# Attention outputs kept features by tokens through DRAM, with SyncE's queue in program order

## The chip, the cores and the metric

The kernel runs on one core of one Trainium2 chip. The metric is the device time of one execution in microseconds (us). Three runs of the kernel before took 2798.26, 2801.53 and 2804.0 us; their median, 2801.53 us, is the time that the change is measured against. A profile is one further execution under the hardware profiler.

## The reference

One transformer block on 2048 tokens of 576 features, all in float32. Six modulation rows come from a silu of a condition vector and a matrix. The block is attention with 32 heads of 18 features, then a gated unit of 4608 hidden features:

```python
h = _layernorm(x) * (1 + ca) + sa
q, k, v = (h @ wqkv) split into 32 heads of 18
p = softmax(q @ k.T * 18 ** -0.5)
x = x + ga * ((p @ v) laid side by side @ wo)
h = _layernorm(x) * (1 + cb) + sb
x = x + gb * ((sigmoid(h @ w_gate) * (h @ w_up)) @ w_down)
```

## The kernel before

The program has three stages. The first (to about 245 us) normalizes the input, and projects queries, keys and values; queries and keys go to DRAM (`qd`, `kd`) as two float32r parts. The second is attention (to about 1534 us). The third is the gated unit, a Strassen-like scheme of seven products a block in two halves of the tokens.

**Attention** is a loop over 32 units (L1039). A unit `u` is one half of the queries (1024 of them, `half`) and one pair of heads (`p`); it has 16 steps `kt`, one for each 128 keys. A step has four score products of 128 keys by 512 queries (L1084, "t" in the code), each followed by an exponential on ScalarE (L1088), and takes the four value products of the step two before it (`values`, L656), which add up an output `o` of 128 rows: four groups of 32 (two heads by two blocks of 512 queries), of which the first 18 rows are features and row 18 (`DH`) is the sum of the exponentials. Between them stand four more score products the other way round (L550, "m"), whose row maxima VectorE takes (L556 to L561). These maxima run ahead: the first "m" for unit `u + 2` comes at step 10 of unit `u` (64 a unit, and 24 ahead at the start). When a unit's maxima are complete, `spread` (L577) transposes them and SyncE writes them into four rows of the queries' tile (`mrows`), so that the score products subtract them.

Two steps make a pair. The order of TensorE's products in a pair is written out by hand in the strings of `STEPS`: "V" is a whole value product of 512 columns, "A" and "B" its two halves, "K" takes the finished output, "G" makes room for one piece of the work on rows (`rows0`, `rows1`), "S" for the spread, "O" for the transposes of the output. A pair whose piece is heavy (18 or 28 more products) takes the order "full"; at steps 2 and 12 the heavy piece is held back. TensorE and ScalarE run in the order written (`tc.manual_schedule`); the other engines' queues, SyncE's among them, are ordered by a planner that works from estimated costs. A queue works in order: an instruction that waits holds what stands behind it.

**Loads of a unit.** At the start of unit `u`, `load_heads(u + 2)` (L499) issues eight DMAs on SyncE's queue: for each of the two heads 54 rows of queries (L514, L517) and 54 rows of keys (L518, L522). The tiles that they overwrite are those of unit `u - 1`.

**A unit's output.** At step 1 of the next unit `taken` (L668) copies `o` to `oT` on ScalarE (L673). At step 2, `outputs` (L676) turns it in four transposes on TensorE (L683), ScalarE copies the result back (L699), VectorE takes 16 inverses a row (L702), and GpSimd scales 2 x 144 elements a row (L705) into `Oa` or `big`, which hold tokens by features.

**Rows.** `project_o` (L761) takes 128 tokens at a time. It turns their features back (L772 and L789, four and one transposes, or three for the second half's tokens), splits them into two float32r parts, and multiplies them by the output weights (L805). The first half's eight blocks of rows go from unit 15 on, with the second layer norm behind them (`first_rows`, L871); the second half's from unit 27 on, with the first 384 features only. The last 192 features of these rows go to DRAM (`oend`) and are turned and multiplied in the gated unit's stage (`last_rows`, L1511, transposes at L1526 and L1534), in which VectorE's order too is by hand.

**Other work in attention.** GpSimd prepares the down-projection's weights (`down_parts`) in units 4 to 14 and moves them by DMAs of its own queue; in units 1 and 3, 2.6 MB of modulation weights are loaded on SyncE's queue (`load_mod`, L126).

Of the kernel before, what the change touches and what calls it, by code (L numbers as in the profile page):

```python
# [15 lines left out]
F32 = mybir.dt.float32  # L16
# [71 lines left out]
def tile_block(ctx, tc, x_in, wqkv, wo, w_gate, w_up, w_down, c_in, w_mod, out):  # L88
# [206 lines left out]
    oend = dram.tile([P, 8, D - DL], F32, name="oend")  # L295
# [338 lines left out]
    Os = [Oa]  # L634
# [33 lines left out]
    def taken():  # L668

        if "whole" in state:  # L670
            half, p, acc = state.pop("whole")
            oT = epool.tile([P, 512], F32, name="oT")
            nc.scalar.copy(oT, acc)  # L673
            state["end"] = (half, p, oT)

    def outputs():  # L676

        if "end" not in state:
            return
        half, p, oT = state.pop("end")  # L680
        tp = bank().rearrange("p (b q) -> p b q", q=P)
        for b in range(4):
            nc.tensor.transpose(tp[:, b, :], oT[:, b * P : (b + 1) * P], ident)  # L683

        yield
        tq = tp.rearrange("p b (j e) -> p j b e", e=32)
        rec = epool.tile([P, 4, 4], F32, name="rec")
        if half == 1 and p == H // 2 - 1:
            nc.vector.reciprocal(rec, tq[:, :, :, DH])
            state["last"] = epool.tile([P, 512], F32, name="oT")[:, 0 : 16 * DH].rearrange("p (t e) -> p t e", t=8)  # L690
            for h in range(2):
                nc.vector.tensor_tensor(
                    state["last"][:, :, h * DH : (h + 1) * DH].rearrange("p (c b) e -> p c b e", c=2),
                    tq[:, 2 * h : 2 * h + 2, :, 0:DH],
                    rec[:, 2 * h : 2 * h + 2, :].unsqueeze(3).to_broadcast([P, 2, 4, DH]),
                    op=ALU.mult,
                )
            return
        nc.scalar.copy(oT, tp.rearrange("p b q -> p (b q)"))  # L699
        yield  # L700
        tq = oT.rearrange("p (b j e) -> p j b e", j=4, e=32)
        nc.vector.reciprocal(rec, tq[:, :, :, DH])  # L702
        for h in range(2):
            f0 = (2 * p + h) * DH
            nc.gpsimd.tensor_tensor(  # L705
                Os[half][:, :, f0 : f0 + DH].rearrange("p (c b) e -> p c b e", c=2),
                tq[:, 2 * h : 2 * h + 2, :, 0:DH],
                rec[:, 2 * h : 2 * h + 2, :].unsqueeze(3).to_broadcast([P, 2, 4, DH]),
                op=ALU.mult,
            )  # L710


# [4 lines left out]
    def load_wo():  # L717
# [31 lines left out]
        for _ in range(4):  # L749
            yield  # L750
# [3 lines left out]
    def project_o(t):  # L754

        wo_h, wo_l, we = weights
        if t <= 8:
            held_rows[:] = temp([P, 2048], F32R), temp([P, 2048], F32)
        T, T_ = held_rows
        if t < 8:  # L760
            xt, full, od = T_[:, 0:D], T_[:, 1024:1536], T_[:, 1536:1664]  # L761
        else:
            T, T_ = T[:, 1024 * (t % 2) : 1024 * (t % 2) + 1024], T_[:, 960 * (t % 2) : 960 * (t % 2) + 960]
            xt, full = T_[:, 0:D], T_[:, D : D + 384]
        nc.gpsimd.dma_start(xt, x_rows[:, t, :])
        src = Os[t // 8][:, t % 8, :]
        n = 4 if t < 8 else DL // P
        oh = T[:, 0 : n * P]
        ol = T[:, 512 : 512 + n * P]
        pt = bank()  # L770
        for i in range(n):
            nc.tensor.transpose(pt[:, i * P : (i + 1) * P], src[:, i * P : (i + 1) * P], ident)  # L772
        if t >= 12:
            nc.vector.tensor_copy(oh, pt[:, 0 : n * P])
            nc.vector.tensor_sub(ol, pt[:, 0 : n * P], oh.bitcast(F32))  # L775
        else:
            full = full[:, 0 : n * P]
            nc.vector.tensor_copy(full, pt[:, 0 : n * P])
            nc.gpsimd.tensor_copy(oh, full)
            nc.gpsimd.tensor_sub(ol, full, oh.bitcast(F32))  # L780
        yield None if t < 8 else "g"
        if t < 8:
            om = T[:, 1024:1152]
            omh = T[:, 1152:1280]
            nc.gpsimd.tensor_copy(
                od.rearrange("p (a e) -> p a e", e=64), src[:, DM:D].unsqueeze(1).to_broadcast([P, 2, 64])
            )
            pt = bank()
            nc.tensor.transpose(pt[:, 0:P], od, ident)  # L789
            nc.vector.tensor_copy(od, pt[:, 0:P])  # L790
            nc.gpsimd.tensor_copy(om[0:64], od[0:64])
            nc.gpsimd.tensor_copy(omh[64:P], od[64:P])
            nc.gpsimd.tensor_sub(om[64:P], od[64:P], omh[64:P].bitcast(F32))
            yield "g"
        for h in range(2):
            cols = slice(h * HALF, (h + 1) * HALF)
            ts_ = []
            for i in range(n):
                a, b = oh[:, i * P : (i + 1) * P], ol[:, i * P : (i + 1) * P]
                ts_ += [(a, wo_h[:, i, cols]), (a, wo_l[:, i, cols]), (b, wo_h[:, i, cols])]  # L800
            if t < 8:
                ts_ += [(om, we[:, 0, cols]), (om, we[:, 1, cols])]
            acc = bank()
            for i, (a, w) in enumerate(ts_):
                nc.tensor.matmul(acc[:, :HALF], a, w, start=i == 0, stop=i == len(ts_) - 1)  # L805
            to = Oa[:, t, :] if t < 8 else xt
            nc.vector.tensor_add(to[:, cols], xt[:, cols], acc[:, 0:HALF])
            yield None if h else "g"
        if t >= 8:
            nc.gpsimd.dma_start(x1p[:, t - 8, :], xt)  # L810
# [64 lines left out]
    def first_rows():  # L875
        yield from load_wo()
        for t in range(8):
            yield from project_o(t)
# [118 lines left out]
    def last_rows_project():  # L997
        for t in range(8, NT):
            yield from project_o(t)

# [33 lines left out]
    manual.enter_context(tc.manual_schedule(engines={mybir.EngineType.PE, mybir.EngineType.Activation}))  # L1034
    follow = []
    rows0 = first_rows()
    rows1 = last_rows_project()
    downs = down_parts()
    for u in range(UNITS):  # L1039
        half, p = divmod(u, H // 2)  # L1040
        qs, ks = heads(u)
        if 0 < u < UNITS - 2:
            load_heads(u + 2)
        if u == H // 2:
            Os.append(big.tile([P, 8, 640], F32, name="big"))
        for kt in range(NT):
# [3 lines left out]
            if kt % 2 == 0:  # L1050
                heavy = state.get("next") == "g"
                hold = heavy and (kt == 2 or kt == 12 and u < UNITS - 1)
                halved = step >= 10 and (hold or not heavy)
                rows = FROM0 <= step < FROM1
                order = two_steps(STEPS["full" if not halved else "rows" if rows else kt if kt in STEPS else "half"])
# [78 lines left out]
    for _ in outputs():  # L1134
        pass
# [375 lines left out]
    def last_rows():  # L1511

        def psum():
            return pd.tile([P, 512], F32, name="d")
# [303 lines left out]
```

## Time and profile before

| what | value |
|---|---|
| runs | 2798.26, 2801.53, 2804.0 us |
| the profiled execution | 2804.88 us |
| its span | 2803.1 us |
| granted TensorE clock, mean | 0.998 |
| TensorE matmul busy | 2771.9 us (99%) |
| VectorE busy | 2306.3 us (82%) |
| ScalarE busy | 1609.3 us (57%) |
| GpSimd busy | 814.6 us (29%) |

The page gives an engine's busy time over the whole span, though the stages differ: ScalarE is nearly full in attention and half idle in the gated unit. Matmul ends are modelled, so a busy share of 99% doesn't say how close TensorE is to its peak; the distance from one value product to the same one a pair later does, since these starts are recorded. "PEld" is TensorE's load of weights, "SPq" SyncE's queue, in which only the issue of a DMA is seen and not its landing. A row of the profile reads: start or count, duration, engine, line, operation, tiles written and read.

### The profile page before, as it was taken

What the parts mean: (1) busy time and instruction counts of PE and PEld (TensorE: products, weight loads), DVE (VectorE), ACT (ScalarE), POOL (GpSimd) and SP (SyncE); (2) the same over time, 40 slices, a digit from 0 to 9 for tenths busy, and PEclk for the clock granted to TensorE, in tenths of its full rate; (3) what the DMA queues carried; (4) which work ended last, traced back from release to release, by engine and by line L of the source; (5) the groups of instructions that cost most, each with busy time, mean ns of one, the idle gap of its engine ahead of it and who ended that gap; (6) DMA issues with size and microseconds to landing.
All of it is one profiled execution on the core that took longest, in us unless ns stands there. A gap on an engine that the chain in (4) does not pass through costs nothing.

```text
span 2803.1 us, 50644 instructions
## 1 busy us (share of the span) xinstructions
PE 2771.9 (99%) x18637; PEld 1847.4 (66%) x18637; DVE 2306.3 (82%) x4370; ACT 1609.3 (57%) x3051; POOL 814.6 (29%) x1077
## 2 busy tenths in 40 slices
PE   7999999999999999999999999999999999999999
PEld 5975444444444444444444888888888888888888
DVE  7278999999998888999883778888898677777777
ACT  3215999999999878999888332333333222222221
POOL 3125207888843111663103222232221100000000
PEclk9999999999999999999999999999999999999999
DMA  5344224444432120232127766667767956566653
GB/s 172 121 157 140 78 61 162 171 169 166 172 133 82 36 58 24 98 106 71 43 68 227 273 222 223 240 213 273 278 245 280 339 195 201 194 200 195 200 195 120
DMA packets 170777, 462.59 MB, mean 165 GB/s; under 512 B 21212, under 2 KB 88032, under 8 KB 160416
## 3 DMA queue, kind: packets, MB, share of 16 engines
q1 hardware_dynamic: 150064, 360.72, 38.4%
q0 software_dynamic: 20464, 98.62, 9.9%
q8 instruction: 147, 2.41, 0.4%
q14 instruction: 102, 0.84, 0.1%
HBM read 281.92 MB, written 176.82 MB: 164 GB/s over the span
## 4 chain that ended last, share of the span: by engine, by line
PE 92%; DVE 4%; DMA 2%; issue 2%; POOL 0%; ACT 0%; SPq 0%; DVEq 0%; ACTq 0%; POOLq 0%
PE x L1225 26%; PE o L656 19%; PE s L1084 12%; PE s L550 11%; PE d L1375 8%; PE d L1307 6%; PE s L336 4%; PE s L805 2%; PE s L389 1%; DMA out_dram<-Oa 1%; DVE mx L556 1%; PE s L683 1%; DMA wq_raw<-in_A_wqkv_dram 1%; DVE w L1215 0%; DVE Oa L1379 0%
## 5 line engine op out<-in xcount | busy, mean ns | idle before, releaser
L1088 ACT ACTIVATE p<-s 128x512 f32<-128x512 f32 x2048 | 1069.1, 616 | 89.2 <-PE s L1084 62.6
L556 DVE TENSOR_REDUCE mx<-s 128x1 f32<-128x512 f32 x1568 | 1000.9, 683 | 101.3 <-PE s L550 75.1
L656 PE MATMUL o<-p,vaug 128*32 128x256 f32 (+1 forms) x5848 | 595.1, 478 | 0.1
L550 PE MATMUL s<-k,q 54*128 54x512 f32 x1920 | 548.6, 434 | 2.0 <-DVE t L775 1.0
L1084 PE MATMUL s<-q,k 56*128 56x512 f32 x1920 | 527.7, 440 | 0.0
L550 PEld LDWEIGHTS s<-k,q 54*128 54x128 f32 x1920 | 273.4, 184 | 231.9 <-DVE mx L561 88.0
L1084 PEld LDWEIGHTS s<-q,k 56*128 56x128 f32 x1920 | 249.8, 184 | 232.1 <-ACT p L1088 72.9
L1225 PE MATMUL x<-k,w 128*128 128x512 f32 x1512 | 370.0, 392 | 0.0
L1225 PEld LDWEIGHTS x<-k,w 128*128 128x128 f32 x1512 | 276.8, 188 | 53.3 <-PE o L656 0.8
L1375 PE MATMUL d<-wd,hh 128*128 128x288 f32 x1248 | 249.9, 295 | 2.4 <-DVE Oa L1379 2.4
L656 PEld LDWEIGHTS o<-p,vaug 128*32 128x32 f32 x5848 | 116.2, 108 | 203.1 <-issue 187.5
L1225 PE MATMUL x<-big,w 128*128 128x512 f32 x1008 | 245.5, 392 | 0.7 <-DVE u L1724 0.7
L1225 PE MATMUL x<-w,w 128*128 128x512 f32 x1008 | 245.3, 391 | 0.0
L1225 PEld LDWEIGHTS x<-big,w 128*128 128x128 f32 x1008 | 185.1, 188 | 37.0 <-DVE u L1724 1.1
L1225 PEld LDWEIGHTS x<-w,w 128*128 128x128 f32 x1008 | 184.3, 188 | 34.5
L1375 PEld LDWEIGHTS d<-wd,hh 128*128 128x128 f32 x1248 | 202.2, 188 | 6.2 <-DVE Oa L1379 3.1
L1375 PE MATMUL d<-wd,hl 128*128 128x288 f32 x624 | 184.3, 295 | 0.0
L1379 DVE TENSOR_TENSOR Oa<-Oa,d 128x288 f32<-128x288 f32 x312 | 136.6, 453 | 55.1 <-PE d L1375 51.2
L561 DVE CUSTOM_DVE_ANT_0 over<-s,over 128x512 f32<-128x512 f32 x240 | 163.9, 683 | 1.3 <-PE s L1084 1.2
L559 ACT ACTIVATE over<-s 128x512 f32<-128x512 f32 x240 | 145.8, 608 | 11.3 <-PE s L550 9.3
L1234 ACT ACTIVATE sg<-x 128x512 f32<-128x512 f32 x36 | 21.6, 599 | 210.2 <-PE x L1225 210.2
L1206 ACT CAST w<-S 128x768 fp32r<-128x768 f32 x71 | 59.4, 836 | 137.8 <-POOL S L1179 136.0
(275 smaller groups left out, 3898.5 us busy)
## 6 DMA issues: line engine op xcount, KB each, us to landing
ws<-w SPq DMA_DIRECT2D x126, 640.0 KB
w<-ws SPq DMA_DIRECT2D x126, 640.0 KB
wd<-wds SPq DMA_DIRECT2D x19, 1152.0 KB
k<-kd SPq DMA_DIRECT2D x60, 360.0 KB
wds<-w POOLq DMA_DIRECT2D x18, 1152.0 KB, 5.2
wtd<-t POOLq DMA_DIRECT2D x32, 576.0 KB, 5.0
wt<-wtd SPq DMA_DIRECT2D x64, 288.0 KB
wd<-wds SPq DMA_DIRECT2D x52, 288.0 KB
```

Of the source, the lines that this page charges most:

```text
L336: nc.tensor.matmul(acc, w, hT[:, t, cols], start=n == 0, stop=n == len(ts_) - 1)
L550: nc.tensor.matmul(sp, qs[rows, qt * P : (qt + 1) * P], ks[rows, at * 512 : (at + 1) * 512], start=True, stop=True,)
L556: nc.vector.tensor_reduce(to, sp, axis=AX.X, op=ALU.max)
L559: nc.scalar.activation(over, sp, AF.Relu)
L561: nc.vector.tensor_tensor_reduce(out=over, in0=sp, in1=over, scale=1.0, scalar=LOWEST, op0=ALU.add, op1=ALU.max, accum_out=mx[:, h * n + q ...
L656: nc.tensor.matmul(acc[32 * j : 32 * j + 32, cols], vaug[:, kt, (2 * p + h) * VW : (2 * p + h) * VW + 32], probs[2 * c + h][:, cols], star ...
L1084: nc.tensor.matmul(sT, ks[rows, kcols], qs[rows, c * 512 : (c + 1) * 512], start=True, stop=True)
L1088: state["exp"] = nc.scalar.activation(pr, sT, AF.Exp, scale=SCALE)
L1225: nc.tensor.matmul(acc[v], w[:, v, a, :], X[s][:, b, :], start=first and n == 0, stop=n == 6, skip_group_check=not first,)
L1307: nc.tensor.matmul(acc, a[:, rows], w[:, k, :], start=n == 0, stop=n == 2)
L1375: nc.tensor.matmul(acc[:, :HALF], a[:, f, rows], w[:, f, cols], start=n == 0, stop=n == 5)
L1379: nc.vector.tensor_add(Oa[:, t, cols], Oa[:, t, cols], acc[:, :HALF])
```

## The change

The output stays features by tokens, and the transposes on both sides of it go.

- `taken` still copies `o` to `oT`. It then stores the four rows of sums in DRAM (`osums`) and loads them as 128 x 16 (`sT`).
- `outputs` is a new generator. From step 2: VectorE inverts the 128 x 16, SyncE stores them in DRAM and loads them spread out, 32 rows for each group (`R`, 128 x 512). From step 6 GpSimd multiplies `R` by `oT`, in place. From step 14 SyncE stores the four groups of 18 rows in `ot`, a DRAM tensor of 576 features by 2048 tokens.
- `load_rows` brings `ot` back as features by tokens into `big`, at units 14, 16, 26 and 27. `rows_parts` splits 128 tokens' columns of it on GpSimd, one block of rows ahead of its products; `project_rows` replaces `project_o`.
- The orders for steps 2 and 4 are taken out of `STEPS`, and heavy pieces are held back at step 12 alone.
- SyncE is added to the engines in program order, and `load_heads(u + 2)` moves from a unit's start to behind its step 4.
- The last unit's output goes to DRAM whole (`lastd`); `last_rows` loads features by tokens, takes the last sums' inverses, and has no transposes.

```diff
-        if 0 < u < UNITS - 2:
-            load_heads(u + 2)
-        if u == H // 2:
-            Os.append(big.tile([P, 8, 640], F32, name="big"))
+        if u in (14, 26):
...
+            load_rows(u // 26, range(3) if u == 14 else range(2))
...
-                hold = heavy and (kt == 2 or kt == 12 and u < UNITS - 1)
+                hold = heavy and kt == 12 and u < UNITS - 1
...
             pending.append((half, p, kt, probs))
+            if kt == 4 and 0 < u < UNITS - 2:
+                load_heads(u + 2)
...
-    manual.enter_context(tc.manual_schedule(engines={mybir.EngineType.PE, mybir.EngineType.Activation}))
+    manual.enter_context(
+        tc.manual_schedule(engines={mybir.EngineType.PE, mybir.EngineType.Activation, mybir.EngineType.SP})
+    )
```

The new end of a unit:

```python
    def taken():
        ...
        nc.scalar.copy(oT, acc)
        if half == 1 and p == H // 2 - 1:
            nc.sync.dma_start(lastd, oT)
            return
        sT = epool.tile([P, 16], F32, name="sT")
        to = osums[half * H // 2 + p, 0]
        nc.sync.dma_start(to, oT[DH::32, :])
        nc.sync.dma_start(sT, to.rearrange("j (q r) -> (j q) r", r=16))
        follow.append(outputs(half, p, oT, sT))

    def outputs(half, p, oT, sT):
        while state["kt"] < 2:
            yield
        rec = epool.tile([P, 16], F32, name="rec")
        paced(nc.vector.reciprocal(rec, sT))
        to = osums[half * H // 2 + p, 1]
        nc.sync.dma_start(to.rearrange("j (q r) -> (j q) r", r=16), rec)
        R = state["room"] if "room" in state else bgp.tile([P, 512], F32, name="R")
        nc.sync.dma_start(R, to.unsqueeze(1).to_broadcast([4, 32, 512]))
        yield
        while state["kt"] < 6:
            yield
        paced(nc.gpsimd.tensor_mul(R, oT, R))
        yield
        while state["kt"] < (8 if state["u"] == UNITS - 1 else 14):
            yield
        for h in range(2):
            for c in range(2):
                f0, n0, j = (2 * p + h) * DH, half * HW + c * 512, 2 * h + c
                nc.sync.dma_start(ot[f0 : f0 + DH, n0 : n0 + 512], R[32 * j : 32 * j + DH, :])
```

The new rows, cut to what is multiplied and when:

```python
    def rows_parts(t):
        ...
        nc.gpsimd.dma_start(xt, x_rows[:, t, :])
        src = state["rows"][:, 0:n, cols]
        ...
        nc.gpsimd.tensor_copy(oh3, src)
        nc.gpsimd.tensor_sub(ol3, src, oh3.bitcast(F32))
        ...

    def project_rows(t0):
        if t0:
            for _ in range(5):
                yield
        ahead = rows_parts(t0)
        yield
        yield "g"
        for t in range(t0, t0 + 8):
            n, oh, ol, om, xt = ahead
            for h in range(2):
                ...
                if h == 0 and t < t0 + 7:
                    ahead = rows_parts(t + 1)
                ...
                yield "g" if t < t0 + 7 or h == 0 else None
```

In `last_rows` the loads and the split now read (for each 512 tokens):

```diff
-                od = pool.tile([P, 4, 256], F32, name="od")
-                nc.sync.dma_start(od[:, :, 0:192], oend[:, t0 : t0 + 4, :])
-                nc.sync.dma_start(od[:, :, 192:256], oend[:, t0 : t0 + 4, 128:192])
-                yield 1.4, 5 if t0 == 0 else 2
-                pt = psum()
-                for j in range(4):
-                    nc.tensor.transpose(pt[:, j * P : (j + 1) * P], od[:, j, 0:P], ident)
...
+                nc.gpsimd.memset(R, 1.0)
+                for p0 in (0, 64):
+                    p1 = p0 + 64 - 2 * DH
+                    nc.sync.dma_start(end[p0:p1], ot[DM : D - 2 * DH, n0 : n0 + 512])
+                    for h in range(2):
+                        j, p2 = 2 * h + c, p1 + h * DH
+                        nc.sync.dma_start(end[p2 : p2 + DH], lastd[32 * j : 32 * j + DH, :])
+                        nc.sync.dma_start(R[p2 : p2 + DH], to[j : j + 1, :].to_broadcast([DH, 512]))
+                yield 1.1, 3 if t0 == 0 else 2
...
+                nc.vector.tensor_mul(end, end, R)
```

More of the change, by code (lines that the diff above doesn't have):

```diff
@@ L668, in taken @@
     def taken():
[L670 to L678, printed above, removed]
-            return
[L680 to L683, printed above, removed]
-        yield
[L686 to L699, printed above, removed]
@@ new lines, in taken @@
+        if "whole" not in state:
+            return
+        half, p, acc = state.pop("whole")
+        oT = epool.tile([P, 512], F32, name="oT")
+        nc.scalar.copy(oT, acc)
+        if half == 1 and p == H // 2 - 1:
+            nc.sync.dma_start(lastd, oT)
+            return
+        sT = epool.tile([P, 16], F32, name="sT")
[3 more added lines that the diff above has]
+        follow.append(outputs(half, p, oT, sT))
@@ L748, in load_wo @@
         weights.extend((wo_h, wo_l, we))
-        for _ in range(4):
+        for _ in range(10):
             yield
     held_rows = []
-    def project_o(t):
-        wo_h, wo_l, we = weights
[L757 to L810, printed above, removed]
@@ L876, in first_rows @@
         yield from load_wo()
-        for t in range(8):
-            yield from project_o(t)
+        yield from project_rows(0)
         for t in range(8):
@@ L1061, in tile_block @@
                     taken()
-                elif does in "OSG":
-                    if halved and kt == 2:
-                        follow.append(outputs())
-                        next(follow[-1], None)
+                elif does in "SG":
                     if "spread" in state:
@@ L1133, in tile_block @@
     taken()
-    for _ in outputs():
-        pass
     manual.close()
-    nc.sync.dma_start(oend[:, :, D - DL - 2 * DH :], state["last"])
     att.close()
@@ L1518, in last_rows @@
             nc.gpsimd.dma_start(w, wod)
[L1519 to L1526 removed]
+            sT = pool.tile([P, 16], F32, name="sT")
```

107 lines of the change are left out of this document (81 added, 26 removed), and 2 rows, old and new, of the table STEPS.

## The prediction

> **What bounds the kernel now.** I read the page's busy line and its chain first, then the windows of the three stages.
>
> ```profile
> PE 2771.9 (99%) x18637; PEld 1847.4 (66%) x18637; DVE 2306.3 (82%) x4370; ACT 1609.3 (57%) x3051; POOL 814.6 (29%) x1077
> PE 92%; DVE 4%; DMA 2%; issue 2%; POOL 0%; ACT 0%; SPq 0%; DVEq 0%; ACTq 0%; POOLq 0%
> 270.00:1534.00 1264.00, 1261.00 (x10316) 549.98 (x10313) 1113.37 (x2126) 1169.13 (x2333) 553.88 (x824) 1.00 0.32 105
> 1545.00:2803.00 1258.00, 1249.57 (x6886) 1102.75 (x6884) 1009.93 (x1887) 348.51 (x557) 170.40 (x168) 1.00 0.66 227
> ```
>
> The chain runs through TensorE for 92%. In attention (the first window; its columns are length, then PE, PEld, DVE, ACT, POOL, clock, DMA share, GB/s) ScalarE too is busy for 1169 of 1264 us: two engines are nearly full. Which of them sets a pair's length, the timeline of one unit tells. These are the whole value products that open the pairs of steps 0, 2, 4, 6, 8 and 10 of unit 10, and what stands extra in them:
>
> ```profile
> 624.93 1.07 PE L656 MATMUL o<-p,vaug 128*32 128x512 f32 x8
> 628.90 0.63 ACT L673 COPY oT<-o 128x512 f32<-128x512 f32 x1
> 629.73 1.06 PE L656 MATMUL o<-p,vaug 128*32 128x512 f32 x8
> 631.62 0.66 PE L683 MATMUL s<-ident,oT 128*128 128x128 f32 x4
> 632.80 0.65 ACT L699 COPY oT<-s 128x512 f32<-128x512 f32 x1
> 635.06 1.07 PE L656 MATMUL o<-p,vaug 128*32 128x512 f32 x8
> 639.67 1.06 PE L656 MATMUL o<-p,vaug 128*32 128x512 f32 x8
> 644.35 1.07 PE L656 MATMUL o<-p,vaug 128*32 128x512 f32 x8
> 648.98 1.07 PE L656 MATMUL o<-p,vaug 128*32 128x512 f32 x8
> ```
>
> The pairs take 4.80, 5.33, 4.61, 4.68 and 4.63 us. The pair with four transposes is 0.70 longer than a plain one (4.63). The pair of step 0 has ScalarE's extra copy of 0.63 us and grows by 0.17 alone. So extra work on TensorE lengthens a pair in full, on ScalarE by a quarter: **TensorE is the bound**, with ScalarE close behind. A transpose costs 0.70/4 = 0.175 us there.
>
> **What is removed.** TensorE loses 4 x 32 transposes of outputs, 5 x 8 and 3 x 8 of rows, and 16 in the last rows.
>
> ```profile
> L683 PE MATMUL s<-ident,oT 128*128 128x128 f32 x128 | 20.9, 286 | 0.1
> L702 DVE RECIPROCAL rec<-oT 128x16 f32<-128x16 f32 x31 | 7.8, 252 | 15.8 <-ACT oT L699 15.4 <-issue 0.4
> L772 PE MATMUL s<-ident,Oa 128*128 128x128 f32 x32 | 5.2, 287 | 0.2
> L772 PE MATMUL s<-ident,big 128*128 128x128 f32 x24 | 4.4, 292 | 0.0
> 1559.92 0.60 PE L1526 MATMUL d<-ident,od 128*128 128x128 f32 x4
> ```
>
> In attention that is 128 + 64 = 192 transposes by 0.175 = 33.6 us. In the gated unit's stage four take 0.60 in the row, so 16 take 2.4. Together **36.0 us**. By busy time alone (20.9/128 = 0.163 each) the 192 would come to 31.3; I take the pair's price, since it has the gaps. ScalarE loses its copy of 0.65 in the same pair, so that it doesn't become the bound in TensorE's place. The heavy products are the same, 16 heavy pairs for each half of the rows before and after. They come closer together, at 0 cost: a heavy pair is TensorE's own sum already. GpSimd's split of the next rows is then due two pairs ahead; it is 29% busy and has room. If that cover failed, a block would wait for GpSimd's few us, 16 times.
>
> **What is added, off TensorE.** GpSimd's 128 x 512 product takes the place of two 128 x 144 ones. It is due at step 6 and used at step 14, so it costs nothing. VectorE loses the copies at L778 and L790 and keeps an inverse of 16 columns. In the last rows two 128 x 512 products and an inverse come onto VectorE, busy for 1010 of 1258 us there: hidden, unless a DMA they wait for is late (0 to 10 us; I take 0, since the loads are issued two and three products of the stage ahead).
>
> **What is moved: the heads' loads.** SyncE's queue now runs in program order. In a unit it holds four new DMAs ahead of the eight loads: sums to DRAM (needs the copy L673), sums back (needs the first landed), inverses to DRAM (needs VectorE, which needs the second landed), inverses back (needs the third landed). The words "step 4" hold nothing back: SyncE gets to the loads when the fourth DMA is issued, which is three landings behind the copy. The trace has one such write and read back through DRAM, and one store with its landing:
>
> ```profile
> 403.32 0.52 SPq L198 DMA_DIRECT2D gates<-w  x2
> 406.31 0.36 SPq L199 DMA_DIRECT2D gb_b<-gates  x1
> 325.06 0.51 SPq L198 DMA_DIRECT2D gates<-w  x2
> 330.54 0.35 SPq L199 DMA_DIRECT2D ga_b<-gates  x1
> x1p<-t POOLq DMA_DIRECT2D x8, 288.0 KB, 2.4
> ```
>
> SyncE's read behind its own write is issued 3.0 us after the pair of writes began (2.7 after the second), and 5.5 when a large load is in flight. GpSimd's store of 288 KB lands in 2.4. The new transfers are 8 KB: I take 2.2 a landing, near that store. As bounds I use 1.5 (an estimate: 288 KB at the 165 GB/s that the page gives as mean take 1.7 of the 2.4 us, so a small one may be much quicker) and 3.0.
>
> The copy ends 628.90 + 0.63 - 624.93 = 4.6 us into the unit. With three landings (6.6), the inverse (0.25 in the row of L702, and some 0.4 behind a maximum on VectorE) and the fourth issue (0.36) **the loads begin at 12.2**; before, they began 0.3 before the unit. When must they have landed, and how long do they take?
>
> ```profile
> 649.97 0.18 PEld L550 LDWEIGHTS s<-k,q 54*128 54x128 f32 x1
> 650.55 0.22 DVE L568 TENSOR_REDUCE nm<-mx 128x16 f32<-128x64 f32 x1
> 1085.31 1.65 SPq L514 DMA_DIRECT2D q<-qd  x2
> 1090.05 0.48 SPq L522 DMA_DIRECT2D k<-kd  x1
> 1095.00:1097.00 2.00, 2.00 (x18) 0.73 (x16) 1.73 (x4) 1.97 (x5) 0.29 (x1) 1.00 0.45 104
> 1097.00:1099.00 2.00, 2.00 (x26) 0.84 (x22) 1.89 (x4) 2.00 (x5) 0.00 (x0) 1.00 0.01 5
> 547.77 0.78 SPq L514 DMA_DIRECT2D q<-qd  x1
> 564.00:566.00 2.00, 2.00 (x20) 1.15 (x18) 1.96 (x6) 1.95 (x5) 0.00 (x0) 1.00 0.24 93
> 566.00:568.00 2.00, 2.00 (x22) 0.89 (x22) 1.75 (x4) 2.00 (x5) 1.45 (x2) 1.00 0.00 0
> 433.00:816.00 383.00, 383.00 (x3252) 165.35 (x3250) 356.67 (x670) 374.11 (x751) 298.53 (x479) 1.00 0.49 172
> 1085.00:1321.00 236.00, 235.79 (x1999) 97.63 (x1998) 219.70 (x416) 224.55 (x450) 120.14 (x144) 1.00 0.24 83
> ```
>
> The last reduction of unit 11's maxima stands at 650.55, so the product at 649.97 is the first for unit 12, out of tiles that unit 10 loaded: it comes 25.0 us into the unit, 24.3 once the pair of step 2 is 0.70 shorter. It is of head 1, whose loads are the last four, so it needs all eight. In unit 21 nothing else moves data: from the first issue at 1085.31 the traffic goes on into the window at 1095 and is over just after 1097, some 12.4 us with the landing. In unit 8 GpSimd's weights move as well, and the traffic from 547.77 on ends shortly before 566: up to 17.5 us. The last two rows show for how long that holds: a DMA share of 0.49 in units 5 to 14 against 0.24 from unit 21 on. For units 5 to 14 I take 15, the middle. The 256 KB of inverses ahead in the rings add some 0.5.
>
> So the loads are **late**: 12.2 + 0.5 + 12.4 - 24.3 = 0.8 us in the quiet units (15, 16, 20 to 27: ten, 8 us), and 12.2 + 0.5 + 15 - 24.3 = 3.4 in units 5 to 14 (34 us). TensorE works in order: the late maximum holds the score products behind it, and ScalarE, with an exponential or two in hand, starves. Units 17 to 19, 28 and 29 have heavy pairs ahead of step 10 and aren't touched:
>
> ```profile
> 943.29 1.06 PE L656 MATMUL o<-p,vaug 128*32 128x512 f32 x8
> 973.60 1.06 PE L656 MATMUL o<-p,vaug 128*32 128x512 f32 x8
> big<-in_w_mod_dram SPq DMA_DIRECT2D x4, 1152.0 KB
> ```
>
> (step 10 of unit 18 comes after 30.3 us.) In units 1 and 3 the modulation weights, 2.6 MB, now go out behind the last maxima's rows and ahead of the four DMAs: some 5 us more each, 10 us. The row loads of units 14 and 16 stand ahead likewise: 3. VectorE waits for the second landing at the inverse, in front of its maxima: 31 x 0.2 = 6, with what the banks don't cover. Sum 61 us.
>
> **The sum** against the profiled execution: 2804.9 - 36.0 + 61 = 2830 us; that execution is 3.4 above the median of the runs shown (2801.5), so 2827 by the median.
>
> The Trainium skill, "DMA: Bandwidth & Descriptors", section "Anatomy of one DMA — SWDGE (gpsimd) path", gives a fixed cost of about 2.0 us for a DMA, most of it the receipt of the write, and so speaks against three landings in a row. The trace agrees roughly: 2.4 for the store. By it the loads would begin 0.6 us sooner, and the sum would be some 12 us lower.
>
> **The rivals.**
>
> *The loads are in time.* For it: at 1.5 us a landing they begin at 10.1 and land at 23.0 in a quiet unit, before 24.3. Units 5 to 14 are then late by up to 1.3, units 1 and 3 by 3: 0 to 19 us back out of 36. Time 2766 to 2785, say 2775; faster. Against it: the row of 3.0.
>
> *The delay just eats the gain*: 36 us in all, at about 1.8 a landing; 2796 to 2807.
>
> *VectorE is held by the inverse instead.* The maxima stand behind it in the queue. If the planner put it where its estimate has the sums landed and they come 2 us later, the seven banks fill (16 products a pair of 4.63: seven in 2.0 us) and TensorE stands. It decides from 36/31 = 1.2 us a unit on; at 2 us it gives 2801.5 - 36 + 62 = 2828, with the loads in time. For it: VectorE is busy for 1113 of 1264 us. Against: the planner knows a DMA takes time.
>
> **How the numbers follow.** Loads late: 0.58, own range 2808 to 2864. VectorE held: 0.08, slower as well. Gain eaten: 0.09. Loads in time: 0.25. Thus faster by over 0.2% (5.6 us, about what a measurement of this kernel can tell from no change) 0.25, within it 0.09, slower 0.66. At 3.0 us a landing the sum would reach 2880; leaving a tenth out there, and little below the rival in time, the range is 2768 to 2864.
>
> **What would show it.** The pair of step 2 at 4.6 us proves the gain. For the forecast: the loads' issues some 12 us into a unit, and TensorE idle at the first maximum of step 10 behind a DMA into `k` or `q`, more in units 5 to 14 than from 20 on, and none in 17 to 19. Waits of VectorE before the inverse show the third rival. I'm wrong if step 10's pair keeps 4.63 us throughout, or if landings take 1.5 us.

## Result, and the profile after

The change makes the kernel slower: 2909.88 us (median of 4 runs, 2904.97 to 2913.8) against 2799.9 us (4 runs of the kernel before, 2796.65 to 2804.0), a ratio of 1.039 with a 95% interval of 1.037 to 1.041. The profiled execution took 2908.63 us, its span 2906.8 us. The prediction had the sign and the mechanism, but only a quarter of the loss.

From the page of the changed kernel, the busy line, the chain, and the group of the products for the maxima; then that group in the kernel before; then, of the changed kernel again, the window of attention that was shown of before:

```profile
PE 2795.9 (96%) x18429; PEld 1842.0 (63%) x18429; DVE 2293.2 (79%) x4342; ACT 1598.0 (55%) x3020; POOL 831.2 (29%) x1048
PE 80%; DMA 12%; DVE 4%; SPq 1%; issue 1%; ACT 1%; POOL 1%; DVEq 0%; ACTq 0%; POOLq 0%
L550 PE MATMUL s<-k,q 54*128 54x512 f32 x1920 | 570.5, 449 | 76.4 <-DMA k<-kd 73.9
```

```profile
L550 PE MATMUL s<-k,q 54*128 54x512 f32 x1920 | 548.6, 434 | 2.0 <-DVE t L775 1.0
```

```profile
270.00:1534.00 1264.00, 1184.79 (x9344) 506.63 (x9340) 1046.02 (x1991) 1063.52 (x2115) 551.22 (x764) 0.95 0.33 108
```

TensorE ran 208 instructions fewer (18429 against 18637) and yet was busy for longer, 2795.9 us against 2771.9. Two things changed: the chain now goes through DMAs for 12% of the span (2% before), and TensorE waited 73.9 us for `k<-kd`, the heads' keys; and the granted clock in attention (the third number from the end) is 0.95, where it was 1.00.

Both are seen in one unit. These are the value products that open the pairs of steps 0, 2 and 4 of unit 6, then TensorE's rows around its step 10, in the timeline of the changed kernel (start, duration, what ran, and in brackets the wait before it):

```profile
485.89 1.06 PE L655 MATMUL o<-p,vaug 128*32 128x512 f32 x8
490.71 1.07 PE L655 MATMUL o<-p,vaug 128*32 128x512 f32 x8
495.39 1.07 PE L655 MATMUL o<-p,vaug 128*32 128x512 f32 x8
...
509.30 1.07 PE L655 MATMUL o<-p,vaug 128*32 128x512 f32 x8
...
517.40 0.76 PE L550 MATMUL s<-k,q 54*128 54x512 f32 x1 [6.60 <-DMA k<-kd]
...
523.69 1.93 PE L655 MATMUL o<-p,vaug 128*32 128x512 f32 x8
```

The pairs of steps 0 and 2 take 4.82 and 4.68 us (4.80 and 5.33 in unit 10 before): the transposes' 0.65 us are gained. The pair of step 10 takes 523.69 - 509.30 = 14.39, where it takes 4.66 to 4.69 in a plain unit before. Of the excess of 9.7, the wait explains 6.6. The rest lies behind it: the eight value products that open the next pair take 1.93 us, not 1.07. The windows of this stretch (length; busy time of PE, PEld, DVE, ACT, POOL; granted clock, DMA share, GB/s) show it:

```profile
509.60:513.02 3.42, 1.20 (x9) 0.18 (x1) 1.47 (x5) 1.76 (x4) 3.42 (x7) 1.00 0.59 205
513.02:516.43 3.41, 0.00 (x0) 0.00 (x0) 0.00 (x0) 0.00 (x0) 3.33 (x6) 0.50 0.16 61
516.43:519.84 3.41, 2.44 (x13) 1.06 (x13) 1.48 (x3) 1.09 (x2) 3.41 (x6) 0.50 0.00 0
519.84:523.26 3.42, 3.42 (x22) 1.53 (x18) 1.51 (x3) 1.80 (x4) 3.42 (x7) 0.50 0.50 205
523.26:526.67 3.41, 3.41 (x18) 1.03 (x14) 1.83 (x5) 1.64 (x4) 2.45 (x5) 0.50 0.76 314
526.67:530.08 3.41, 3.41 (x35) 1.35 (x35) 2.96 (x6) 3.26 (x8) 0.83 (x2) 1.00 0.92 315
```

The clock is halved for four windows of 3.41 us, of which TensorE spent more than two at work again.

SyncE's queue in the same unit shows why the keys are late:

```profile
490.52 0.54 SPq L679 DMA_DIRECT2D osums<-oT  x1
492.25 0.35 SPq L680 DMA_DIRECT2D sT<-osums  x1
494.94 0.34 SPq L690 DMA_DIRECT2D osums<-rec  x1
499.38 0.58 SPq L692 DMA_DIRECT2D R<-osums  x1
500.01 0.78 SPq L514 DMA_DIRECT2D q<-qd  x1
```

The first load is issued 14.1 us into the unit (500.01 - 485.89), behind all four DMAs of the sums. The first landing took 1.7 us (490.52 to 492.25), the third 4.4 (494.94 to 499.38).

Over all units, from the starts of the value products: the pairs of steps 10 and 12 together grew by 128 us against before, the others shrank by 17. By the landings in the trace, the loads came 80 us late in all (beyond the moment, 24.4 us into a plain unit, at which TensorE asks for them); the other 48 us come on top of that. About 5 of the 48 belong to unit 19, whose loads are in time: there the products for the maxima stand behind the layer norm of the rows on VectorE, which waits for GpSimd, and a score product of TensorE waits for them:

```profile
1113.30 0.50 PE L1077 MATMUL s<-q,k 56*128 56x512 f32 x1 [3.35 <-DVE mx L556]
```

### The profile page after: what moved, and what is told of

It reads as the page before. It is cut to its first block, busy times and chain, and to the rows that moved or that the text cites. A ratio compares the mean times of both kernels' runs of the same rounds, so it can differ in the third digit from the quotient of the medians.

```text
span 2906.8 us, 50780 instructions
## 1 busy us (share of the span) xinstructions
PE 2795.9 (96%) x18429; PEld 1842.0 (63%) x18429; DVE 2293.2 (79%) x4342; ACT 1598.0 (55%) x3020; POOL 831.2 (29%) x1048
## 4 chain that ended last, share of the span: by engine, by line
PE 80%; DMA 12%; DVE 4%; SPq 1%; issue 1%; ACT 1%; POOL 1%; DVEq 0%; ACTq 0%; POOLq 0%
PE x L1221 25%; PE o L655 14%; PE s L1077 10%; PE s L550 9%; PE d L1371 7%; DMA k<-kd 7%; PE d L1303 6%; PE s L336 3%; PE s L799 2%; DMA R<-osums 2%; PE s L389 1%; DMA osums<-rec 1%; ACT p L1081 1%; DMA wd<-wds 1%; DVE mx L556 1%
## 5 line engine op out<-in xcount | busy, mean ns | idle before, releaser
L550 PE MATMUL s<-k,q 54*128 54x512 f32 x1920 | 570.5, 449 | 76.4 <-DMA k<-kd 73.9
L655 PE MATMUL o<-p,vaug 128*32 128x256 f32 (+1 forms) x5848 | 619.1, 495 | 0.0
L1077 PE MATMUL s<-q,k 56*128 56x512 f32 x1920 | 555.1, 454 | 6.8 <-DVE mx L556 3.4
L550 PEld LDWEIGHTS s<-k,q 54*128 54x128 f32 x1920 | 287.4, 192 | 301.3 <-issue 88.8
L1077 PEld LDWEIGHTS s<-q,k 56*128 56x128 f32 x1920 | 261.3, 192 | 270.0 <-DVE mx L556 82.8
```

The costliest lines, as they stand in the source:

```text
L550: nc.tensor.matmul(sp, qs[rows, qt * P : (qt + 1) * P], ks[rows, at * 512 : (at + 1) * 512], start=True, stop=True,)
L655: nc.tensor.matmul(acc[32 * j : 32 * j + 32, cols], vaug[:, kt, (2 * p + h) * VW : (2 * p + h) * VW + 32], probs[2 * c + h][:, cols], star ...
L1077: nc.tensor.matmul(sT, ks[rows, kcols], qs[rows, c * 512 : (c + 1) * 512], start=True, stop=True)
```

## The experiments

Each ratio is against runs of the kernel before on the same chip.

**1. The loads back at a unit's start**, all else as changed:

```diff
+        if 0 < u < UNITS - 2:
+            load_heads(u + 2)
...
-            if kt == 4 and 0 < u < UNITS - 2:
-                load_heads(u + 2)
```

> The changed kernel with the heads' loads back at a unit's start, ahead of the four DMAs of the inverses on SyncE's queue. Theory A (the loads land after step 10 of a unit needs them; the waits come to 80 us, and TensorE's clock, which the profile shows halved for some us behind each long wait, costs another 55): the pair of step 10 takes 4.65 us again in every unit, and the time is that of the kernel before less the 36 us of transposes, about 2765 us, plus whatever the sums cost that now land behind the loads. Rival B (VectorE is held by the inverse in front of its maxima): the sums land some 8 us later than in the changed kernel, so VectorE waits more, about 5 us in each of 30 units, and the time stays above 2900 us. Rival C (the new transfers themselves, 256 KB of inverses a unit, slow everything): about 2900 us, as before the move.

Measured: 2782.06 us, ratio 0.995 (0.993 to 0.997), faster than both kernels. The group of the maxima's products, then TensorE's two largest waits in attention (total, times, longest):

```profile
L550 PE MATMUL s<-k,q 54*128 54x512 f32 x1920 | 552.0, 437 | 0.9 <-DVE mx L556 0.9
```

```profile
PE o L655 <- ACT oT L673: 6.1, 2, 5.4
PE s L1079 <- DMA q<-mrows: 6.0, 4, 1.9
```

The wait for keys is gone altogether, and the sums' chain behind the loads holds nobody in turn. The move of eight DMAs in one queue is worth 128 us. What is left stands in three places: unit 4, unit 16 (pairs of 10.10 and 8.19 us at steps 0 and 2) and unit 31 (10.33 at step 0). In unit 16, ScalarE's copy waits for the one `oT` tile, which GpSimd still reads. GpSimd's timeline:

```profile
851.46 1.42 POOL L729 TENSOR_TENSOR t<-t,ga_b 128x576 f32<-128x576 f32 x1 [2.88 <-DMA t<-in_A_wo_dram]
...
856.70 1.27 POOL L696 TENSOR_TENSOR R<-oT,R 128x512 f32<-128x512 f32 x1
```

Its product L696 stands behind the loads of the output weights, 8.2 us into the next unit (which begins at 848.5).

**2. The loads between the second and the third DMA.**

```diff
-            if kt == 4 and 0 < u < UNITS - 2:
+            if kt == 1 and 0 < u < UNITS - 2:
```

> The changed kernel with the heads' loads behind step 1, so that they stand between the load of the sums and the store of the inverses. They begin some 6.5 us into a unit instead of 11 to 16, and need 14 to 17 us. Theory A: they land at 21 to 24 us, step 10 needs them at 24.4, so that waits are left in the busiest of units 5 to 14 alone, 0 to 2 us; the time is 2770 to 2790 us. Rival B: the sums are ahead of the loads, so that VectorE gets its inverse as early as in the changed kernel, and nothing changes: about 2910 us. Rival C: about 2910 us.

Measured: 2800.03 us, ratio 1.000 (0.999 to 1.001). That is some 10 us slower than expected. The waits for keys are gone, but the inverse, on VectorE in front of the maxima, now holds TensorE in six places. TensorE's first wait and VectorE's in front of the inverse:

```profile
PE s L550 <- DVE mx L556: 8.6, 6, 3.2
```

```profile
DVE rec L688 <- ACT p L1081: 13.1, 7, 5.2
DVE rec L688 <- DMA sT<-osums: 6.5, 3, 4.0
```

This is the prediction's third rival, in another kernel: it needs the sums to land late while the planner puts the inverse early. In experiment 1 the planner knew the loads to be ahead of the sums and put the inverse some 25 us into the unit.

**3. The kernel before with late loads alone**: `load_heads` moved behind step 4, and each of its DMAs held by that step's last exponential (SyncE's order is still the planner's).

```diff
-        if 0 < u < UNITS - 2:
-            load_heads(u + 2)
...
+            if kt == 4 and 0 < u < UNITS - 2:
+                load_heads(u + 2, paced)
```

> The kernel before, with its transposes and its own outputs, and one thing changed: each of the eight loads of a unit also waits for the last exponential of step 4, so that they begin about 13.5 us into a unit. Nothing else of the change is in it: no inverses by DMA, no wait of VectorE for a DMA. Theory A: they land at 26 to 31 us and step 10 needs them at 25.0, so waits of 1 to 6 us in the units without heavy pairs, with the halved clock behind the long ones: 2860 to 2900 us. Rivals B and C: what makes the changed kernel slow isn't in this one; 2800 to 2815 us.

Measured: 2902.46 us, ratio 1.038 (1.036 to 1.040), just above the 2860 to 2900 expected. TensorE's largest wait:

```profile
PE s L550 <- DMA k<-kd: 49.4, 22, 5.7
```

Late loads need nothing else of the change to cost over 100 us. In the profiled execution (span 2886.6 us) they are 56 us late by their landings, and the pairs of steps 10 and 12 grew by 88 us: again more than the lateness.

**4. Experiment 1 with the inverse from step 8 and the product from step 12**, the last unit excepted.

```diff
-        while state["kt"] < 2:
+        while state["kt"] < (2 if state["u"] == UNITS - 1 else 8):
...
-        while state["kt"] < 6:
+        while state["kt"] < (6 if state["u"] == UNITS - 1 else 12):
```

> The changed kernel with the loads at a unit's start, the inverse taken from step 8 on instead of 2, and the product on GpSimd from step 12 on instead of 6 (in the last unit as before). Theory A: no load is late, and no sum is waited for: the gain alone is left, 2765 us (2760 to 2775). Rival C: the transfers are all there, so about 2900 us. Against the run with the loads first and the inverse at step 2 it tells what the inverse's place costs: the same time if VectorE isn't held there, up to 150 us less if it is.

Measured: 2802.51 us, ratio 1.002 (1.000 to 1.003); 2765 were expected. TensorE's two largest waits:

```profile
PE o L655 <- ACT oT L673: 10.1, 4, 5.7
PE s L1079 <- DMA q<-mrows: 10.0, 3, 8.1
```

A later product frees `oT` later, and the stores of it, in SyncE's order, then hold the next unit's rows. What waited for VectorE now waits for GpSimd.

**5. Experiment 1 with its three places mended.** In unit 15 VectorE takes the product, at step 14; the gated unit's first weights are loaded from step 3 of unit 30 instead of 7; two loads of its inputs are held until step 9 of unit 31.

```diff
-        while state["kt"] < 6:
+        late = state["u"] == 15
+        while state["kt"] < (14 if late else 6):
             yield
-        paced(nc.gpsimd.tensor_mul(R, oT, R))
-        yield
+        paced((nc.vector if late else nc.gpsimd).tensor_mul(R, oT, R))
+        if not late:
+            yield
...
-            if u == 30 and kt == 7:
+            if u == 30 and kt == 3:
...
+        if n in (2, 3):
+            paced(load)
```

> The changed kernel with the loads at a unit's start (2782.06 us in the first experiment), and three things moved that waited there: in unit 15 VectorE instead of GpSimd scales the output, at step 14; the first weights of the gated unit are loaded from unit 30's step 3 instead of 7; and two 1.3 MB loads of inputs are held until unit 31's step 9. Theory (the left-over of the first experiment is GpSimd's queue in unit 15 and DMA contention with the maxima's rows in unit 30): unit 16's pairs of steps 0 and 2 go from 10.10 and 8.19 to 4.7 and 4.9, -8.7 us; unit 31's from 10.33 and 5.65 to 4.5 and 4.5, -7.0; together 2766 us. Rival (what was late is replaced by the next, the inverses or the stores behind the later product): within 5 us of 2782.

Measured: 2775.42 us (6 runs), ratio 0.992 (0.991 to 0.994), the fastest kernel here that leaves nothing out. Unit 16's pairs are 4.69 and 4.85 us, unit 31's 4.21 and 4.19: both stalls went. The time is 9 us above what was expected. Unit 4 still loses 2.7 us at its step 0 (7.52), and what follows attention took 1269.2 us, where it took 1264.9 in experiment 1.

**6. Work for TensorE while it waits.** Sixteen products with the running unit's own tiles, which are there already, are put in front of the waiting one, in units 5 to 13, into the bank that it then starts afresh.

```diff
+                if i == 0 and 7 <= u < 16:
+                    q2, k2 = heads(u - 2)
+                    for _ in range(16):
+                        nc.tensor.matmul(sp, q2[rows, 0:P], k2[rows, 0:512], start=True, stop=True)
```

> The changed kernel, with 16 products more in front of the product that waits for the loaded keys, in units 5 to 13: the same operands' rows of the unit before, already there, into the bank that the waiting product then starts afresh, so that TensorE works while it waits. Theory (behind an idle stretch the clock is halved for some microseconds, and this is what the lateness cost beyond itself): the value products behind the waits take 1.07 us again instead of 1.93, and of the nine units' 59.5 us of excess over 4.65 and 4.97 in the pairs of steps 10 and 12 about 20 go, less some microseconds where a wait was shorter than the 16 products (units 7, 8, 11): 2885 to 2895 us although work was added. Rival (the halved clock belongs to something else, or is only in the records): no gain, and the added products cost 0 to 15 us: 2909 to 2925.

Measured: 2902.08 us, ratio 1.038 (1.036 to 1.039), 7.8 us under the changed kernel though 144 products were added. 15 to 25 were expected, and the intervals of the two ratios overlap, so the time alone settles nothing. The units tell more. Unit 9 is the clean pair: the keys land 29.1 us into the unit in the changed kernel and 29.0 us here. The changed kernel first, then this one (the sixteen are L553, the waiting product L554):

```profile
642.72 1.07 PE L655 MATMUL o<-p,vaug 128*32 128x512 f32 x8
648.45 0.76 PE L550 MATMUL s<-k,q 54*128 54x512 f32 x1 [4.23 <-DMA k<-kd]
654.74 1.85 PE L655 MATMUL o<-p,vaug 128*32 128x512 f32 x8
660.50 1.07 PE L655 MATMUL o<-p,vaug 128*32 128x512 f32 x8
```

```profile
648.40 1.07 PE L659 MATMUL o<-p,vaug 128*32 128x512 f32 x8
649.40 4.00 PE L553 MATMUL s<-k,q 54*128 54x512 f32 x16
654.06 0.49 PE L554 MATMUL s<-k,q 54*128 54x512 f32 x1 [0.67 <-DMA k<-kd]
657.67 1.06 PE L659 MATMUL o<-p,vaug 128*32 128x512 f32 x8
662.63 1.07 PE L659 MATMUL o<-p,vaug 128*32 128x512 f32 x8
```

From the value products of step 10 to those of step 14 it is 17.78 us without, and 14.23 with the filling: 3.55 us less for the same landing. What is left above the plain pairs of steps 10 and 12 (14.23 against 9.63) is 4.6 us, just what the keys were late by. In units 6, 7, 10 and 13, whose waits are longer than the filling, there is half clock behind the wait.

**7. No sums' chain**, with the loads still behind step 4.

```diff
-        nc.sync.dma_start(to, oT[DH::32, :])
-        nc.sync.dma_start(sT, to.rearrange("j (q r) -> (j q) r", r=16))
...
-        paced(nc.vector.reciprocal(rec, sT))
-        to = osums[half * H // 2 + p, 1]
-        nc.sync.dma_start(to.rearrange("j (q r) -> (j q) r", r=16), rec)
...
-        nc.sync.dma_start(R, to.unsqueeze(1).to_broadcast([4, 32, 512]))
...
-        paced(nc.gpsimd.tensor_mul(R, oT, R))
+        paced(nc.gpsimd.tensor_mul(R, oT, oT))
```

> The changed kernel without the four DMAs and the inverse (the sums are neither stored nor loaded, and GpSimd multiplies the output by itself, so the scaling is left out); the loads stay behind step 4 in the program. Theory (the loads are late because SyncE's queue stands still in front of them, not because of where they are in the program): they issue as soon as the queue is empty, within some 5 us of a unit's start, the step-10 pairs are 4.65, and the time is 2765 to 2780, the removed transposes' gain less what units 16 and 31 lose. Rival (the place behind step 4 itself, or the stores, makes them late): step-10 pairs stay over 6 us and the time over 2850.

Measured: 2773.2 us, ratio 0.991 (0.990 to 0.993). SyncE issues unit 6's first load 0.3 us *before* the unit (which begins at 465.0):

```profile
464.67 0.79 SPq L514 DMA_DIRECT2D q<-qd  x1
```

So "step 4" in the program is no time. The loads come when the queue in front of them is empty.

**8. A short spread.** The fourth DMA brings 8 KB into a tile of its own instead of 256 KB into `R`.

```diff
-        nc.sync.dma_start(R, to.unsqueeze(1).to_broadcast([4, 32, 512]))
+        few = epool.tile([P, 16], F32, name="few")
+        nc.sync.dma_start(few, to[:, 0:16].unsqueeze(1).to_broadcast([4, 32, 16]))
...
-        paced(nc.gpsimd.tensor_mul(R, oT, R))
+        paced(nc.gpsimd.tensor_mul(R, oT, oT))
```

> The changed kernel with all four DMAs, of which the last brings 8 KB into a small tile (128 x 16) instead of 256 KB (128 x 512); GpSimd multiplies the output by itself, so the scaling is left out. The loads' start stays at 11 to 16 us into a unit, behind the same waits. Theory (the spread of the inverses, 5.2 us to its landing in front of the loads, is the mis-sized term of the lateness): the loads take some 2 us less, the lateness of 80 us falls by 35 to 50, and the halved clock behind it by about 20: 2840 to 2860. Rival (as the prediction had it, it costs the loads 0.5 us): 2885 to 2900; the lateness is then the traffic of the other queues.

Measured: 2852.32 us, ratio 1.020 (1.018 to 1.022): 57.6 us less than the changed kernel. The loads begin where they did, at 13.0 us on average over units 1 to 29 in both, but take 13.3 us to land instead of 15.5. The lateness falls from 80 to 36 us. One quiet unit, 23, in the changed kernel and then in this one (the first load's issue, and TensorE's wait):

```profile
1263.15 0.79 SPq L514 DMA_DIRECT2D q<-qd  x1
...
1280.87 1.06 PE L550 MATMUL s<-k,q 54*128 54x512 f32 x3 [4.19 <-DMA k<-kd]
```

```profile
1224.98 0.79 SPq L514 DMA_DIRECT2D q<-qd  x1
...
1240.04 0.74 PE L550 MATMUL s<-k,q 54*128 54x512 f32 x3 [1.40 <-DMA k<-kd]
```

17.7 us from issue to use against 15.1.

**9. The waits filled unit by unit**, 3 to 35 products in twenty units, 271 in all, by the lateness that each had in the changed kernel's trace (`BUSY` is the table of these numbers).

```diff
+                if i == 0 and u >= 2:
+                    q2, k2 = heads(u - 2)
+                    for _ in range(BUSY.get(u - 2, 0)):
+                        nc.tensor.matmul(sp, q2[rows, 0:P], k2[rows, 0:512], start=True, stop=True)
```

> As the 16 products, but as many in each unit as fill its wait in the changed kernel's trace to within 0.8 us, at the 0.23 to 0.25 us that one of them took: 3 to 35 in twenty units, 271 in all; units 6, 10 and 13, where 16 left 4 us of idleness and gained nothing, have 26 to 35. Theory (an idle stretch of some 3 us is what halves the clock behind it): with the waits filled the halved stretches go, some 55 us less whatever the landings then scatter by: 2855 to 2880 us, and the mean granted clock goes from 0.976 to 0.99. Rival (the 16 products' 8 us came from transfers that landed a little earlier, not from the clock): 2895 to 2925, as the products only fill time that was lost anyway.

Measured: 2898.39 us (2888.8 to 2910.33), ratio 1.037 (1.033 to 1.040), hardly below the changed kernel. The mean clock rose to 0.987 in the profiled run, but the time missed what was expected by 18 us and more. Unit 13 has its 35 products, and the keys at 32.6 us where it had them at 33.2. These are its windows:

```profile
814.49:817.90 3.41, 3.41 (x17) 2.68 (x16) 0.11 (x1) 0.44 (x1) 3.41 (x8) 1.00 0.56 172
817.90:821.31 3.41, 3.41 (x16) 2.73 (x15) 0.00 (x0) 0.00 (x0) 3.33 (x6) 1.00 0.25 69
821.31:824.73 3.42, 3.42 (x31) 1.60 (x30) 2.21 (x4) 1.84 (x4) 3.42 (x6) 1.00 0.00 0
```

The clock stays full, and the pairs of steps 10 and 12 take 17.7 us together instead of 21.8, a gain of 4.1 of which the earlier landing explains 0.6. In unit 11 five products left a wait of 0.99 us:

```profile
727.86 0.50 PE L555 MATMUL s<-k,q 54*128 54x512 f32 x1 [0.99 <-DMA k<-kd]
```

```profile
725.74:729.15 3.41, 2.42 (x19) 1.24 (x16) 1.31 (x4) 1.46 (x4) 0.00 (x0) 1.00 0.48 195
729.15:732.57 3.42, 3.42 (x23) 1.53 (x18) 1.98 (x4) 2.01 (x5) 2.27 (x3) 0.50 0.28 62
732.57:735.98 3.41, 3.41 (x16) 1.03 (x14) 1.83 (x5) 1.64 (x4) 3.09 (x5) 0.50 0.73 297
```

One microsecond of idleness, and two windows at half clock behind it. My expectation's threshold of 3 us of idleness was wrong: a wait that isn't filled to the end can cost as much as an open one, and the landings differ by 1 to 2 us between the traces, so a fixed filling meets few of them. By the windows the clock theory stands; as a remedy the filling fails.

**10. The spread in four DMAs** of 32 rows each.

```diff
-        nc.sync.dma_start(R, to.unsqueeze(1).to_broadcast([4, 32, 512]))
+        for j in range(4):
+            nc.sync.dma_start(R[32 * j : 32 * j + 32, :], to[j : j + 1, :].to_broadcast([32, 512]))
```

> The changed kernel with the spread of the inverses as four DMAs of 32 rows (64 KB each) instead of one of 128 rows whose source begins with a dimension of 4; the loads stay behind them. In the kernel with the loads first, where nothing else moves, the one DMA showed a DMA share of 0.24 to 0.26 at 88 to 100 GB/s for about 2.6 us: a quarter of the 16 engines. Theory (it holds four engines for 2.6 us, and the loads' packets on those engines stand behind it): in four parts over all engines it is through in some 0.7 us; three more issues of 0.35 to 0.6 us make the loads begin 1.0 to 1.8 us later, but they land 0.5 to 1 us sooner: 2875 to 2900 us. Rival (the 256 KB cost the loads their length whichever engines move them, or the landing is what counts): the loads land 1 to 1.8 us later by the issues, in twenty late units, with the clock behind it: 2925 to 2950.

Measured: 2884.22 us (5 runs), ratio 1.031 (1.029 to 1.033), 25.7 us under the changed kernel. The four issues take 1.72 us where one took 0.58, and the loads begin 1.1 us later (14.1 on average). They take 13.1 us to land instead of 15.5, much as with the short spread (13.3), so that they land 1.3 us sooner in the unit, and the lateness falls from 80 to 54 us. The same bytes over more engines lengthen the loads no more, apart from the 1.1 us of the issues, which are also a head start for these bytes.

## Why the prediction was right or wrong

**The bound was right, and the gain nearly.** The pair of step 2 fell from 5.33 to 4.68 us (4.63 were forecast), and in the plain units from 15 on only to 4.85. Without late loads (experiment 7) attention, from the first value product to the last, is 1266.8 us long against 1293.0. That is 26.2 of the 33.6 forecast, with 4.7 more lost at unit 31 to `q<-mrows` (pairs of 7.99 and 5.69 us against 4.54 and 4.47 before).

**The mechanism was right.** The loads stand behind three landings in an ordered queue, TensorE idles at the first maximum of step 10, and the loads of units 17 to 19 and 28 with their heavy pairs are in time (those of 29, which I had put with them, came 1.6 us late, and it lost 3.3 us at step 10; what unit 19 lost isn't lateness). I forecast that the loads begin at 12.2; they begin at 11.0 to 16.3, 13.0 on average. That this is so near is in part luck: a quiet landing takes 1.4 to 1.8 us and not 2.2, but in units 5 to 14 some take 4 (the third one in unit 6: 4.4), and the inverse waits its turn on VectorE. Experiments 1, 3 and 7 show that late loads, with the clock behind them, are nearly the whole loss; units 8 and 19 lost some 10 us more to waits for VectorE.

**What failed: the size of the loss, in two terms.** 61 us were forecast, of which lateness 55 (8 + 34 + 10 + 3).

- *The inverses ahead in the rings, "some 0.5".* No row stood behind the 0.5. They cost the loads 2.2 us in each unit (15.5 on average against 13.3 in experiment 8). In the ten units that I called quiet this is all that was off: the loads begin at 12.1 us, as forecast, but take 15.1 and not 12.9, and lateness is 21 us instead of 8. In units 5 to 14 they take 16.5 and not 15.5 and also begin 1.0 us later, and lateness is 48 us instead of 34. Lateness in all is 80 us and not 55. I had counted bytes; by its DMA share (last section) the spread runs on about four of the 16 engines, and that the loads' packets on these stand behind it is what experiment 10 bears out.
- *A term that wasn't there: the clock behind a wait.* I took a late load to cost its lateness. In fact the pairs of steps 10 and 12 lost about 43 us more, at half clock. Experiments 6 and 9 show the cause: the same lateness, with TensorE kept busy, costs 3.55 us less in unit 9 and 3.5 in unit 13. The changed kernel itself shows it too: in units 4, 7, 8, 11, 16, 20 and 27 the loads are 0.4 to 2.6 us late, the clock stays full behind the wait, and these pairs are longer than in experiment 7 by the lateness alone, within 0.5 us.

25 and 43 us are 68 of the 79 us between the sum of 2830 and the profiled 2908.6. The rest lies in the smaller gain and in the stalls of units 8, 19 and 31.

**The rivals.** "In time" needed landings of 1.5 us. The quiet ones were about that, so one of my signs of being wrong was there, but the loads were late all the same: their length, not the landings, decided. "VectorE held" happened in unit 8: the sums' load is issued 3.0 us behind their store there (1.7 in unit 6), VectorE stands idle for 2.1 us in front of the inverse, and the pair of step 4 takes 8.13 us instead of 4.63. It happened in several units only where the queue's order was another one (experiment 2).

What stays open: how much of the loads' remaining lateness in units 5 to 14 (25 us with the short spread) comes from GpSimd's transfers beside them. Taking those out wasn't tried.

## What to carry to other kernels

A DMA that waits for a result holds everything behind it in its queue, so loads with a deadline belong ahead of a round trip through DRAM, whatever step of the program they are written at. Price a stall on TensorE at more than its length, here about 1.5 times over all units (once its length where the clock stayed full), and look at the clock in the windows behind it. Before a DMA is put in front of others, look at how many engines it runs on: its DMA share while it runs alone tells it.

## What the runs showed of the hardware

**The clock.** It changes on a fixed grid of 3.41 us: in five kernels (the changed one and experiments 3, 6, 8 and 9) every stretch between two changes is a whole number of such windows long. I counted the grid's windows from 250 to 1640 us in these by TensorE's busy share: of 43 windows at full clock with a share below 0.5, all were followed by half clock; of 97 between 0.5 and 0.9, 24; of 1758 above, none. Where the line lies in between isn't settled: the rows of unit 11 above show a window with 0.71 busy that lost it, but in the changed kernel's unit 7 one with 0.59 kept it:

```profile
557.39:560.80 3.41, 2.02 (x15) 0.59 (x11) 2.12 (x5) 2.57 (x6) 0.00 (x0) 1.00 0.56 225
560.80:564.22 3.42, 2.64 (x25) 1.15 (x25) 2.13 (x4) 1.77 (x4) 1.79 (x3) 1.00 0.35 106
```

Half clock then lasts for one to four windows. The Trainium skill, "TensorE: Matmul & The Clock Gate", section "HAM oscillation — how this bites in real kernels", gives the rule "no PE-idle gaps >~3.4µs". The grid's 3.41 us agree with its figure; as a limit it doesn't hold here, since 0.99 us was enough in unit 11.

**Engines of a DMA.** In experiment 1's kernel the spread runs alone, issued at 1066.73; in the kernel before, the heads' loads of unit 21 run alone (from 1085.31 on). The windows (DMA share is the last number but one):

```profile
1068.50:1071.10 2.60, 2.60 (x25) 0.90 (x23) 2.23 (x5) 2.60 (x7) 0.00 (x0) 1.00 0.23 87
```

```profile
1090.00:1092.00 2.00, 2.00 (x17) 0.64 (x14) 1.62 (x5) 2.00 (x6) 0.84 (x2) 1.00 0.58 184
1092.00:1094.00 2.00, 2.00 (x18) 0.87 (x16) 1.66 (x3) 2.00 (x6) 0.00 (x0) 1.00 0.54 165
```

0.23 is about four engines of 16 (0.25), 0.54 to 0.58 about nine (0.56). The Trainium skill, "DMA: Bandwidth & Descriptors", section "Why a DMA increments its semaphore by 16 and not by 1", says that a DMA uses the largest number of engines, up to 16, that divides the slowest dimension on both of its sides, and on SyncE's queue the lowest-numbered ones. By that rule it is four for 4 and 128, and nine for 18 and 36, with the four among the nine. The shares agree with the numbers; which engines they are, no run here shows, but that the spread lengthened the loads (experiments 8 and 10) fits.
